# Batch 0's attention by head pairs: an order of work written out by hand in a fused attention and snake-MLP kernel

## The chip, the cores and the metric

The kernel runs on one core of a Trainium2 chip. Its time is the device time of one execution in microseconds (us); the median of four runs of the kernel before is 236.2 us, from 235.82 to 236.86. Lower is better.

## The reference

There are 4 batches, 8 heads, 768 tokens and 64 values per head. Each chunk of 32 queries attends to 8 memory slots, 16 keys to its left, its own 32 and 8 to its right. The 8 heads' outputs, side by side, are a 512-wide row per token, and a two-layer MLP with the activation h + sin(alpha h)^2 / alpha follows. All matrices come in float32; the result is 3072 x 512 float32.

```python
scores = scale * np.matmul(q_c, k_full.transpose(0, 1, 3, 2))
a = np.exp(scores - np.max(scores, axis=-1, keepdims=True))
a = a / (np.sum(a, axis=-1, keepdims=True) + 1e-09)
out[:, :, c_start:c_end] = np.matmul(a, v_full)
...
h = x @ w_in                       # 512 -> 2048
g = h + np.sin(alpha * h) ** 2 / (alpha + 1e-09)
return g @ w_out                   # 2048 -> 512
```

## The kernel before

Everything is in bf16 on the matmul side. The order on every engine is the order of the program text, since the schedule is manual.

A token block is 96 tokens (three chunks); a batch has NJ = 8 blocks. The 128 key rows of a block are the 112 keys around it with 8 memory rows between (partitions 64 to 71 of `vw`, columns 40 to 47 of each 104 in `kTi`). Heads go in 4 pairs, since two heads of 64 values fill 128 partitions.

Loading. All of q, k, v and the weights are loaded by DMAs issued on POOL, which convert to bf16 on the way. Batch 0's q and k come pair by pair (`load_qk_pair`, L100), v block by block with two DMAs each (`load_v`, L121), then the first-layer weights in five pieces, q and k of batch 1, the second-layer weights in two pieces, and v of batch 1 (`load_v_all`, L134). [...] an issue waits until the DMA eight places before it has landed. mem_k and alpha are loaded on SP's queue, mem_v on POOL's.

Transposes. `t_k` and `t_q` (L247, L260) turn a pair's k or q on the PE into a PSUM tile (`turn`, L236); DVE copies k into `kTi` (L249, L255), ACT copies q into `qT` (L262). `put_memk` and `put_memv` place the memory rows. For batch 0 the program (L418) does all four pairs, k and q in turn, with two filler matmuls (`spin`, L167: zeros times zeros, to keep the PE busy) after each.

Attention. `qk_exp(j)` (L266) scores one token block for all 8 heads, 8 matmuls into the two-bank tile `sc`, and takes exp on ACT in three parts of 32 queries (L279); the mask is the per-partition bias, which differs for the first and the last block. `pv` (L286) multiplies by v with a column of ones for the sums; DVE takes the reciprocal (L296) and multiplies (L297) into `x_blk`. `xt` (L304) transposes that block on the PE, and DVE or ACT copies it into `xT` (L313). `burst` (L316) runs the eight blocks one after the other, weighting two steps after scoring.

MLP. For each of 16 slices `ft` of 128 hidden values, `l1` (L339) makes 8 matmuls (L347), Sin on ACT (L359), a square on ACT, DVE or POOL by the letter in `sq` (L362, L368, L364), and a multiply-add on DVE into `gT` (L376). For ft 3, 7 and 11 of batch 0 the two halves go to single-bank tiles (`split`; L356, L372). DVE's part of slice ft is written after the matmuls of slice ft and ahead of those of ft + 1. `l2` (L382) is the second layer: 16 matmuls per 128 tokens (L404), a copy, a store. It is a generator, from which the next batch's attention and first layer take steps between their own (`stream.take`). In batch 0's first layer nothing of it runs yet. After that layer come batch 1's transposes (`pair_up`, L223, on POOL and DVE, then `t_k` and `t_q`).

PSUM has three two-bank buffers (`big`: scores, outputs, hidden tiles) and two one-bank buffers (`smp`: fillers, second-layer outputs, some transposes).

```python
for n in range(2 * HP):
    (t_k if n % 2 == 0 else t_q)(kq[n % 2], n // 2)
    spin(2)
...
sq = ("ADADADADPDPAADAA" if i == 0 else "ADAAPDADADAPADAD")[ft]
```

Of the kernel before, what the change touches and what calls it, by code (L numbers as in the profile page):

```python
# [9 lines left out]
P = 128  # L10
QW = 96
NEG = -30000.0
KW = 856
BF = mybir.dt.bfloat16
F32 = mybir.dt.float32
# [30 lines left out]
def kernel(  # L46
# [46 lines left out]
    memv_st = consts.tile([P, B, H, D], BF, name="memv_st")  # L93
    memk_f = gp.tile([32, H, D], F32, name="memk_f", tag="gT")
    w_in_sb = consts.tile([P, KT, d_ff], BF, name="w_in_sb")
    w_out_sb = consts.tile([P, FT, d_model], BF, name="w_out_sb")
# [23 lines left out]

    def load_v(b, j):  # L121
        vw = vws[b % 2]
        lo = QW * j - 16
        r0 = max(0, -lo)
        nc.gpsimd.dma_start(
            vw[r0:64, :, j, 0:D], v[b, :, lo + r0:lo + 64, :].rearrange("h p d -> p h d")
        )
        n = min(56, S - (QW * j + 48))
        nc.gpsimd.dma_start(
            vw[72:72 + n, :, j, 0:D],  # L130
            v[b, :, QW * j + 48:QW * j + 48 + n, :].rearrange("h p d -> p h d"),
        )

    def load_v_all(b):  # L134

        vw = vws[b % 2].rearrange("p h j c -> p (h j) c")
        vf = v[b].rearrange("h s d -> (h s) d")
        n = H * NJ
        nc.gpsimd.dma_start(
            vw[16:64, :, 0:D],  # L140
            vf.rearrange("(n p) d -> p n d", p=QW)[0:48])
        nc.gpsimd.dma_start(
            vw[72:120, :, 0:D],
            vf.rearrange("(n p) d -> p n d", p=QW)[48:96])
        nc.gpsimd.dma_start(
            vw[0:16, 1:n, 0:D],
            vf.rearrange("(n p) d -> p n d", p=QW)[80:96, 0:n - 1])
        nc.gpsimd.dma_start(
            vw[120:128, 0:n - 1, 0:D],
            vf.rearrange("(n p) d -> p n d", p=QW)[0:8, 1:n])  # L150

# [14 lines left out]

    def spin(n):  # L167

        z = smp.tile([P, 512], F32, name="z", tag="sm")
        for _ in range(n):  # L170
            nc.tensor.matmul(z[:], zeros[:, 0:P], zeros[:])  # L171
# [10 lines left out]
    masks.make_identity(nc, ident[:])  # L182
    for hp in range(1, HP):
        load_qk_pair(0, hp, *kq)
    for b in range(B):
        nc.sync.dma_start(memk_f[NM * b:NM * b + NM], mem_k[b].rearrange("h n d -> n h d"))
    nc.gpsimd.dma_start(memv_st[64:72].rearrange("n b h d -> n (b h) d"),
                        mem_v.rearrange("b h n d -> n (b h) d"))
    for c, (a, e) in enumerate(((0, 16), (16, 56), (64, 120), (120, P), (32, 96), (64, 72))):
# [7 lines left out]
    nc.scalar.copy(memk_bf[:], memk_f[:])  # L197
    for j in range(NJ):
        load_v(0, j)
    with nc.allow_non_contiguous_dma(reason="alpha transpose load"):  # L200
# [26 lines left out]

    state = {"n": 0, "t": 0, "pools": 3}

# [6 lines left out]
    def turn(src, hp):  # L236

        t = t_tile()
        for r in range(6):
            if src.shape[1] == 6:  # L240
                nc.tensor.transpose(t[:, r, :], src[:, r].rearrange("p e d -> p (e d)"), ident[:])  # L241
            else:
                for e in range(2):
                    nc.tensor.transpose(t[64 * e:64 * e + 64, r, :], src[:, 2 * hp + e, r, :], ident[:])
        return t
# [13 lines left out]

    def t_q(qb, hp):  # L260
        t = turn(qb, hp)
        nc.scalar.copy(  # L262
            qT[:, hp, :].rearrange("p (a r) -> p a r", r=6), t[:].rearrange("p r a -> p a r")
        )

    def qk_exp(j):  # L266
        sc = big.tile([P, 2, 512], F32, name="sc", tag="big")
        for hp in range(HP):
            for e in range(2):
                nc.tensor.matmul(  # L270
                    sc[:, e, QW * hp:QW * hp + QW],
                    kTi[64 * e:64 * e + 64, hp, 104 * j:104 * j + P],
                    qT[64 * e:64 * e + 64, hp, QW * j:QW * j + QW],
                )
        pt = pts[state["n"] % NPT]
        state["n"] += 1
        for m in range(3):
            col = ((1 if j == 0 else 0), 4, (2 if j == NJ - 1 else 3))[m]
            nc.scalar.activation(  # L279
                pt[:, 0:H * QW].rearrange("p (g e c) -> p e g c", g=4, e=2)[:, :, :, 32 * m:32 * m + 32],  # L280
                sc[:, :, 0:4 * QW].rearrange("p g (e c) -> p g e c", e=4)[:, :, :, 32 * m:32 * m + 32],
                ACTF.Exp, bias=biasm[:, col:col + 1], scale=0.125,
            )
        return pt

    def pv(b, j, pt):  # L286
        x_blk = blk.tile([QW, H, D], BF, name="x_blk")
        rinv = blk.tile([QW, H], F32, name="rinv")
        ot = big.tile([P, 2, 512], F32, name="ot", tag="big")
        otv = ot[:, :, 0:4 * (D + 1)].rearrange("p g (e c) -> p g e c", e=4)  # L290
        for h in range(H):
            nc.tensor.matmul(  # L292
                otv[:, h // 4, h % 4, :], pt[:, QW * h:QW * h + P], vws[b % 2][:, h, j, 0:D + 1]
            )
# [8 lines left out]

    def xt(xT, j, x_blk, ot):  # L304
        if ot is None:
            xtp = smp.tile([P, KT, QW], BF, name="xtp", tag="sm")[:]
        else:
            xtp = ot[:].bitcast(BF)[:, 0, 640:640 + KT * QW].rearrange("p (k c) -> p k c", k=KT)
        for kt in range(KT):
            nc.tensor.transpose(  # L310
                xtp[:, kt, :], x_blk[:, 2 * kt:2 * kt + 2, :].rearrange("p e d -> p (e d)"), ident[0:QW, 0:QW]
            )
        (nc.scalar.copy if ot is None and j in (4, 5, 6) else nc.vector.tensor_copy)(  # L313
            xT[:, :, QW * j:QW * j + QW], xtp)

    def burst(b, stream, shares, lag):  # L316

        xT = xp.tile([P, KT, S], BF, name="xT")
        ptl, xbl = {}, {}
        back = lag + (2 if b == 0 else 1)  # L320
        for s in range(NJ + back):
            n = shares[s] if s < len(shares) else 0
            if s < NJ:
                ptl[s] = qk_exp(s)
            if b == 0:
                spin(1 if 3 <= s < NJ else 2)
            stream.take(n // 3, True)
            if 0 <= s - lag < NJ:
                xbl[s - lag] = pv(b, s - lag, ptl.pop(s - lag))
                if b == 0:  # L330
                    xbl[s - lag] = (xbl[s - lag][0], None)
            stream.take((n + 1) // 3, True)
            if 0 <= s - back < NJ:
                xt(xT, s - back, *xbl.pop(s - back))
            stream.take((n + 2) // 3, True)
        return xT


    def l1(i, ft, xT, gT, sq, split=False):  # L339
        if split:  # L340
            hts = [smp.tile([P, 512], F32, name="hs", tag="sm") for _ in range(2)]
        else:
            hT = big.tile([P, 2, 512], F32, name="hT", tag="big")
            hts = [hT[:, 0], hT[:, 1]]
        for kt in range(KT):
            for hf in range(2):
                nc.tensor.matmul(  # L347
                    hts[hf][:, 0:HALF],
                    w_in_sb[:, kt, P * ft:P * ft + P],
                    xT[:, kt, HALF * hf:HALF * hf + HALF],  # L350
                    start=(kt == 0), stop=(kt == KT - 1),
                )
        u = mlp.tile([P, 2, HALF], F32, name="u")
# [63 lines left out]

    for n in range(2 * HP):  # L418
        (t_k if n % 2 == 0 else t_q)(kq[n % 2], n // 2)
        spin(2)  # L420
        if n == 1:
            mt = smp.tile([P, HP, 32], BF, name="mt", tag="sm")
            for hp in range(HP):
                nc.tensor.transpose(
                    mt[:, hp, :],
                    memk_bf[0:32, 2 * hp:2 * hp + 2, :].rearrange("p e d -> p (e d)"),
                    ident[0:32, 0:32])
            nc.vector.tensor_copy(memkT[:], mt[:])
            put_memk(0)
    put_memv(0)  # L430
    nc.vector.reciprocal(inv_alpha[:], alpha_sb[:])
    for c0, c1 in ((0, 256), (256, 512), (512, 1024), (1024, 1536), (1536, 2048)):
        load_w_in(c0, c1)
    kq_next = load_qk(1)
    for c in range(2):
        load_w_out(c)
    load_v_all(1)

    stream = Stream()
    xT = burst(0, stream, (), 2)  # L440
    put_memk(1)

    for i in range(B):
# [19 lines left out]
        for ft in range(FT):  # L463
            sq = ("ADADADADPDPAADAA" if i == 0 else "ADAAPDADADAPADAD")[ft]
            if 1 <= ft:
                stream.take(3 if last else 2)
            if 0 < i < B - 1 and ft in at_ft:
                piece(at_ft[ft])
            if i == 0 and ft == 13:
                pair_to(2)  # L470
            if finish is not None:
                finish()
            finish = l1(i, ft, xT, gT, sq, i == 0 and ft in (3, 7, 11))
        finish()
        stream.add(l2(i, gT, last))
        if not last:
# [16 lines left out]
            if i + 2 < B:  # L493
                load_v_all(i + 2)
                put_memv(i + 2)
# [31 lines left out]
```

## Time and profile before

| | us |
|---|---|
| Median of four runs | 236.2 |
| The profiled execution's own time | 236.38 |
| Its span in the trace | 234.5 |
| Batch 0: first scores on the PE (L270) | 15.24 |
| Batch 0: exps on ACT, first start to last end (L279) | 15.91 to 24.77 |
| Batch 0: first Sin of the first layer (L359) | 29.88 |
| Batch 0: last multiply-add of the first layer ends (L376) | 55.13 |
| Batch 1: first scores on the PE (L270) | 62.04 |

The profile is of one execution. A row of the timeline has the start, the length, the engine, the line, what is written and read, and in brackets the idle time before it with what ended that. In the chain of waits each row is a start, a length and a place, followed back from the last instruction to whatever released it. Granted clock of the PE is 1.0 throughout.

### The profile page before, as it was taken

The numbers are of one execution on the slowest core, as the hardware profiler recorded it, in microseconds if no ns is written. First come the engines' busy times: TensorE is split into PE (matmuls) and PEld (weight loads), VectorE is DVE, ScalarE is ACT, GpSimd is POOL, SyncE is SP. The second block draws the span as 40 slices with busy tenths as digits, with TensorE's granted clock in tenths as the row PEclk, the third lists the DMA queues.
The fourth block names the chain that finished last, engine by engine and source line by source line (L and its number), as shares of the span: only waits on it lengthen the run. The fifth ranks groups of instructions, "written<-read, shape, count | busy, mean of one in ns | idle before, by whom it ended". The sixth has DMA issues, their size and how long they took to land.

```text
span 234.5 us, 4580 instructions
## 1 busy us (share of the span) xinstructions
PE 221.4 (94%) x1841; PEld 122.5 (52%) x1841; DVE 160.4 (68%) x287; ACT 150.2 (64%) x235; POOL 74.0 (32%) x85
## 2 busy tenths in 40 slices
PE   7799999888999999999999999999999999899994
PEld 2345565445545565564455656564555555453453
DVE  5467659999847987988557698978566358775110
ACT  2359689774697297899664787779564676880110
POOL 8889951823942115139300115020000020110000
PEclk9999999999999999999999999999999999999999
DMA  6999999999999910019999101001111110101112
GB/s 69 176 123 88 156 200 203 207 207 128 141 224 194 122 45 0 3 46 139 186 144 107 45 0 48 0 8 39 45 48 45 48 46 0 45 0 48 65 69 89
DMA packets 52500, 21.07 MB, mean 90 GB/s; under 512 B 36480, under 2 KB 49536, under 8 KB 52480
## 3 DMA queue, kind: packets, MB, share of 16 engines
q0 software_dynamic: 46528, 14.43, 73.5%
q1 hardware_dynamic: 5952, 6.37, 8.7%
q8 instruction: 14, 0.23, 0.4%
q14 instruction: 6, 0.05, 0.1%
HBM read 28.91 MB, written 6.29 MB: 150 GB/s over the span
## 4 chain that ended last, share of the span: by engine, by line
PE 64%; DVE 16%; ACT 8%; issue 6%; DMA 2%; POOL 2%; POOLq 1%; DVEq 0%; ACTq 0%
PE o L404 30%; PE hT L347 18%; DVE gT L376 6%; DVE s L368 4%; ACT u L359 3%; PE sc L270 3%; PE ot L292 3%; DMA q_bf<-in_q_dram 2%; DVE x_blk L297 2%; ACT s L362 2%; PE z L171 2%; PE tt_a L241 2%; ACT pt L279 2%; POOL s L364 2%; PE ot L310 2%
## 5 line engine op out<-in xcount | busy, mean ns | idle before, releaser
L404 PE MATMUL o<-w_out_sb,gT 128*128 128x512 bf16 x368 | 98.5, 380 | 1.2 <-DMA w_out_sb<-in_moe_w_out_dram 0.7
L347 PE MATMUL hT<-xT,w_in_sb 128*128 128x384 bf16 x488 | 87.3, 326 | 4.2 <-DVE gT L376 3.8
L376 DVE SCALAR_TENSOR_TENSOR gT<-s,inv_alpha,hT 128x768 bf16<-128x768 f32 x61 | 60.9, 1012 | 23.1 <-ACT s L362 15.0
L359 ACT ACTIVATE u<-hT,alpha_sb 128x768 f32<-128x768 f32 x61 | 54.7, 897 | 25.4 <-PE hT L347 24.3
L347 PEld LDWEIGHTS <-w_in_sb 128*128 128x128 bf16 x512 | 49.3, 98 | 39.3 <-issue 4.9
L404 PEld LDWEIGHTS <-gT 128*128 128x128 bf16 x368 | 31.9, 97 | 27.1 <-DVE gT L376 1.2
L279 ACT ACTIVATE pt<-sc,biasm 128x256 bf16<-128x256 f32 x96 | 37.4, 488 | 12.8 <-PE sc L270 12.7
L364 POOL TENSOR_TENSOR s<-u 128x768 f32<-128x768 f32 x8 | 12.5, 1567 | 76.1 <-ACT u L359 65.8
L362 ACT ACTIVATE s<-u 128x768 f32<-128x768 f32 x32 | 27.0, 843 | 1.3 <-DVE gT L376 0.4
L368 DVE TENSOR_TENSOR s<-u 128x768 f32<-128x768 f32 x24 | 25.9, 1077 | 0.7 <-ACT u L359 0.5
L297 DVE TENSOR_TENSOR x_blk<-ot,rinv 96x512 bf16<-96x512 f32 x32 | 22.0, 687 | 1.1
L223 POOL COPY pr<-q_bf 128x768 bf16<-128x768 bf16 x12 | 10.2, 853 | 38.8 <-PE tt_a L241 25.3
L296 DVE RECIPROCAL rinv<-ot 96x8 f32<-96x8 f32 x32 | 6.4, 201 | 18.2 <-PE ot L292 18.0
L411 DVE COPY o_sb<-o 128x512 f32<-128x512 f32 x12 | 8.3, 688 | 15.5 <-PE o L404 15.4
L413 ACT COPY o_sb<-o 128x512 f32<-128x512 f32 x11 | 6.4, 583 | 17.9 <-PE o L404 17.9
L171 PE MATMUL z<-zeros 128*128 128x512 bf16 x45 | 15.4, 439 | 1.3 <-DVE zeros L165 1.2
L292 PEld LDWEIGHTS <-pt 128*128 128x128 bf16 x256 | 12.1, 97 | 7.5 <-issue 2.7
L292 PE MATMUL ot<-vw,pt 128*128 128x65 bf16 x256 | 13.0, 193 | 0.7 <-ACT pt L279 0.4
L270 PEld LDWEIGHTS <-kTi 64*128 64x128 bf16 x256 | 6.8, 94 | 12.4 <-issue 5.9
L241 PEld LDWEIGHTS <-pr 128*128 128x128 bf16 x144 | 10.1, 98 | 5.2
L270 PE MATMUL sc<-qT,kTi 64*128 64x96 bf16 x256 | 11.4, 205 | 0.8 <-DVE gT L376 0.6
L310 PEld LDWEIGHTS <-x_blk 96*128 96x128 bf16 x128 | 8.5, 97 | 6.0 <-issue 0.7
(70 smaller groups left out, 171.6 us busy)
## 6 DMA issues: line engine op xcount, KB each, us to landing
out_dram<-o_sb SPq DMA_DIRECT2D x23, 256.0 KB, 2.4
k_bf<-in_k_dram POOLq DMA_DIRECT2D x3, 768.0 KB, 9.3
q_bf<-in_q_dram POOLq DMA_DIRECT2D x3, 768.0 KB, 13.1
vw<-in_v_dram POOLq DMA_DIRECT2D x6, 384.0 KB, 17.4
w_out_sb<-in_moe_w_out_dram POOLq DMA_DIRECT2D x2, 1024.0 KB, 24.7
w_in_sb<-in_moe_w_in_dram POOLq DMA_DIRECT2D x3, 512.0 KB, 9.8
k_bf<-in_k_dram POOLq DMA_DIRECT2D x4, 192.0 KB, 5.8
q_bf<-in_q_dram POOLq DMA_DIRECT2D x4, 192.0 KB, 6.1
```

What stands on the lines that cost most here:

```text
L171: nc.tensor.matmul(z[:], zeros[:, 0:P], zeros[:])
L270: nc.tensor.matmul(sc[:, e, QW * hp:QW * hp + QW], kTi[64 * e:64 * e + 64, hp, 104 * j:104 * j + P], qT[64 * e:64 * e + 64, hp, QW * j:QW ...
L279: nc.scalar.activation(pt[:, 0:H * QW].rearrange("p (g e c) -> p e g c", g=4, e=2)[:, :, :, 32 * m:32 * m + 32], sc[:, :, 0:4 * QW].rearra ...
L292: nc.tensor.matmul(otv[:, h // 4, h % 4, :], pt[:, QW * h:QW * h + P], vws[b % 2][:, h, j, 0:D + 1])
L297: nc.vector.tensor_tensor(out=x_blk[:].rearrange("p (g e) d -> p g e d", g=2), in0=otv[0:QW, :, :, 0:D], in1=rv.unsqueeze(3).to_broadcast( ...
L347: nc.tensor.matmul(hts[hf][:, 0:HALF], w_in_sb[:, kt, P * ft:P * ft + P], xT[:, kt, HALF * hf:HALF * hf + HALF], start=(kt == 0), stop=(kt ...
L359: nc.scalar.activation(u[:], hT[:, :, 0:HALF], ACTF.Sin, scale=alpha_sb[:, ft:ft + 1])
L362: nc.scalar.activation(s2[:], u[:], ACTF.Square)
L364: nc.gpsimd.tensor_tensor(out=s2[:], in0=u[:], in1=u[:], op=ALU.mult)
L368: nc.vector.tensor_tensor(out=s2[:], in0=u[:], in1=u[:], op=ALU.mult)
L376: nc.vector.scalar_tensor_tensor(out=gv, in0=s2[:], scalar=inv_alpha[:, ft:ft + 1], in1=hT[:, :, 0:HALF], op0=ALU.mult, op1=ALU.add)
L404: nc.tensor.matmul(o[:], gT[:, ft, P * s:P * s + P], w_out_sb[:, ft, :], start=(ft == 0), stop=(ft == FT - 1),)
```

## The change

Batch 0 no longer runs block by block over all heads. Its 32 cells (4 pairs by 8 token blocks) are grouped into eight units: unit u holds pair u // 2 and token blocks 0 to 3 or 4 to 7. An order string names every step on the PE: `k`, `q` turn a pair, `s` scores and takes exp of a unit, `v` weights it, `x` transposes it, `z` is a number of fillers. The parts:

- v is loaded by pair, four DMAs per pair, with pair 0 ahead of q and k of pairs 2 and 3. The same function with all 64 rows serves the other batches. v of batch 1 is issued at ft 8 of batch 0's first layer instead of before it.
- mem_v is loaded as float32 on SP's queue and cast by ACT.
- q of pairs 1 and 3 is copied by DVE instead of ACT.
- Batch 0's turns stand in `smp` tiles, with the two fillers written into the same tile ahead of the transposes.
- Where the cells of a unit need different biases, an exp is issued in two parts.
- Batch 0's block transposes go into the free part of the unit's output tile; a unit's copy fills 384 tokens of one 128-row slice of `xT`. The last four copies are on ACT.
- The first layer's first slice takes its matmuls half by half (for batch 0 with the last slice of `xT` at the end).
- The squares of batch 0's first layer are placed anew; alpha's reciprocal comes after the attention.

```diff
+ORDER = (
+    "k 0,q 0,memk 0,k 1,s 0,q 1,s 1,memv 0,s 2,k 2,v 0,q 2,s 3,x 0,v 1,k 3,s 4,x 1,q 3,s 5,"
+    "z 1,v 2,s 6,x 2,z 1,v 3,s 7,x 3,z 2,v 4,z 2,v 5,x 4,z 1,v 6,x 5,z 1,v 7,x 6,z 1,x 7"
+)
...
+    def load_v(b, n0, n1):
         vw = vws[b % 2].rearrange("p h j c -> p (h j) c")
         vf = v[b].rearrange("h s d -> (h s) d")
+        vf = vf.rearrange("(n p) d -> p n d", p=QW)
+        for dst, src in (
+            (vw[16:64, n0:n1, 0:D], vf[0:48, n0:n1]),
+            (vw[72:120, n0:n1, 0:D], vf[48:96, n0:n1]),
+            (vw[0:16, n0 + 1:n1, 0:D], vf[80:96, n0:n1 - 1]),
+            (vw[120:128, n0:n1 - 1, 0:D], vf[0:8, n0 + 1:n1]),
+        ):
+            nc.gpsimd.dma_start(dst, src)
...
     load_qk_pair(0, 0, *kq)
     masks.make_identity(nc, ident[:])
-    for hp in range(1, HP):
+    load_qk_pair(0, 1, *kq)
+    load_v(0, 0, 16)
+    for hp in range(2, HP):
         load_qk_pair(0, hp, *kq)
...
-    nc.gpsimd.dma_start(memv_st[64:72].rearrange("n b h d -> n (b h) d"),
-                        mem_v.rearrange("b h n d -> n (b h) d"))
+    nc.sync.dma_start(memv_f[64:72].rearrange("n b h d -> n (b h) d"),
+                      mem_v.rearrange("b h n d -> n (b h) d"))
...
     nc.scalar.copy(memk_bf[:], memk_f[:])
-    for j in range(NJ):
-        load_v(0, j)
+    nc.scalar.copy(memv_st[64:72], memv_f[64:72])
+    for hp in range(1, HP):
+        load_v(0, 16 * hp, 16 * hp + 16)
...
     def turn(src, hp):
-        t = t_tile()
+        if src.shape[1] == 6:
+            t = t_tile()
+        else:
+            z = smp.tile([P, 512], F32, name="z", tag="sm")
+            spin(2, z)
+            t = z[:].bitcast(BF)[:, 0:6 * P].rearrange("p (r c) -> p r c", r=6)
...
-    def qk_exp(j):
+    def qk_exp(cells):
...
+            cols = [((1 if j == 0 else 0), 4, (2 if j == NJ - 1 else 3))[m] for _, j in cells]
+            c0 = 0
+            for c1 in range(1, 5):
+                if c1 < 4 and cols[c1] == cols[c0]:
+                    continue
+                nc.scalar.activation(
+                    pt[:, 0:H * QW].rearrange("p (g e c) -> p e g c", g=4, e=2)[:, :, c0:c1, 32 * m:32 * m + 32],
...
+                c0 = c1
...
+    def first_burst(kq):
+        xT = xp.tile([P, KT, S], BF, name="xT")
+        cells = [[(u // 2, 4 * (u % 2) + c) for c in range(4)] for u in range(8)]
+        ptl, xbl = {}, {}
+        for what, n in [t.split() for t in ORDER.split(",")]:
+            n = int(n)
+            if what == "k":
+                t_k(kq[0], n)
+            elif what == "q":
+                t_q(kq[1], n, nc.vector.tensor_copy if n in (1, 3) else nc.scalar.copy)
...
+            elif what == "s":
+                ptl[n] = qk_exp(cells[n])
+            elif what == "z":
+                spin(n)
+            elif what == "v":
+                xbl[n] = pv(0, cells[n], ptl.pop(n))
+            elif what == "x":
+                hf = n % 2
+                xt(xT[:, n // 2, HALF * hf:HALF * hf + HALF].rearrange("p (k c) -> p k c", k=KT),
+                   *xbl.pop(n), nc.vector.tensor_copy if n < 4 else nc.scalar.copy)
+        return xT
...
+        order = [(kt, hf) for kt in range(KT) for hf in range(2)]
+        if ft == 0 and i == 0:
+            order = [(kt, hf) for hf in range(2) for kt in range(KT - 1)] + [(KT - 1, 0), (KT - 1, 1)]
+        elif ft == 0:
+            order = [(kt, hf) for hf in range(2) for kt in range(KT)]
...
-    load_v_all(1)
...
-    xT = burst(0, stream, (), 2)
+    xT = first_burst(kq)
+    nc.vector.reciprocal(inv_alpha[:], alpha_sb[:])
...
-            sq = ("ADADADADPDPAADAA" if i == 0 else "ADAAPDADADAPADAD")[ft]
+            sq = ("ADAPADAPDADADAAA" if i == 0 else "ADAAPDADADAPADAD")[ft]
...
+            if i == 0 and ft == 8:
+                load_v(1, 0, H * NJ)
```

## The prediction

> **What bounds the kernel now.** I read the page's engine shares first, then the chain of waits over 0 to 70 us (the change touches only batch 0's front and first layer), then the timeline there, then the DMA issues.
>
> ```profile
> PE 221.4 (94%) x1841; PEld 122.5 (52%) x1841; DVE 160.4 (68%) x287; ACT 150.2 (64%) x235; POOL 74.0 (32%) x85
> ```
>
> The PE's 94% is an average. The chain, start and length in us, tells what rules the part concerned:
>
> ```profile
> 2.20 5.84 DMA q_bf<-in_q_dram
> ...
> 14.81 0.81 ACT qT L262
> ...
> 15.91 4.49 ACT pt L279 x12
> ...
> 24.43 0.69 DVE x_blk L297
> ...
> 28.53 1.33 PE hT L347 x7
> ...
> 44.73 1.95 DVE s L368
> ...
> 58.34 0.82 PE o L404 x3
> ```
>
> Five stages: transposes of all four head pairs until 14.8, eight exp blocks on ACT, a tail of weighting, transposing and copying until 28.5, the first layer (L1) that ends on DVE at 55.13, then batch 1's transposes, behind two kTi copies on DVE (57.29 to 58.29), until 58.34. After 62 us the chain is nearly all PE matmuls, so what reaches that point is kept. Timeline rows (start, length) of the ends of these stages:
>
> ```profile
> 15.91 8.86 ACT L279 ACTIVATE pt<-sc,biasm 128x256 bf16<-128x256 f32 x24 [0.31 <-PE sc L270]
> ...
> 29.88 0.90 ACT L359 ACTIVATE u<-hT,alpha_sb 128x768 f32<-128x768 f32 x1 [0.81 <-PE hT L347]
> ...
> 44.39 1.47 POOL L364 TENSOR_TENSOR s<-u 128x768 f32<-128x768 f32 x1 [0.71 <-ACT u L359]
> 44.65 2.02 DVE L368 TENSOR_TENSOR s<-u 128x768 f32<-128x768 f32 x1
> ...
> 54.12 1.01 DVE L376 SCALAR_TENSOR_TENSOR gT<-s,inv_alpha,hT 128x768 bf16<-128x768 f32 x1 [0.52 <-ACT s L362]
> ```
>
> Exp costs 0.369 each when packed (8.86/24); the last ends at 24.77, and 5.1 us pass until the first Sin, at 29.88: that tail is what can be shortened. The DVE square at 44.65 takes 2.02 where the group's median is 0.95: it started while POOL squared. The loads:
>
> ```profile
> k_bf<-in_k_dram POOLq DMA_DIRECT2D x4, 192.0 KB, 5.8
> vw<-in_v_dram POOLq DMA_DIRECT2D x7, 64.0 KB, 2.8
> vw<-in_v_dram POOLq DMA_DIRECT2D x7, 56.0 KB, 3.4
> ```
>
> By issue plus landing time, k and q land at 5.4, 8.0, 9.1, 10.1, 11.0, 12.0, 12.9, 14.0: 0.99 apart at the end. v's 16 DMAs go out at 8.6 to 21.9, about 0.7 of issue each, and land 2.7 later: POOL's issuing paces them, the engines don't. The first w_in lands at 26.6, the last w_out at 55.2, where PE waits 0.66 for it.
>
> [...] 2.02 against 0.95 above; three squares beside v issues (32.62, 106.69, 110.21) took 0.95. [...] The load here (27.79) is 1.28 and Sin waits for the PE, not for it; [...]
>
> **The change part by part.**
>
> *Loads.* v is now issued per head pair (4 DMAs), pair 0 ahead of k2, q2, k3, q3, and mem_v leaves POOL for SP. The queue never runs dry: each issue is 4 us ahead of its turn. The rate of v with a full queue I take from batch 1's v: 55.2 to 64.8, 9.6 us with a store among it, so 2.1 to 2.4 per pair; I take 2.3. From q1 at 10.1: v0 12.4, k2 13.4, q2 14.4, k3 15.4, q3 16.3, v1 18.6, v2 20.9, v3 23.2, w_in 24.5 (2.1 earlier), the last w_out about 53.2. POOL's waits for the DMA eight places back are met in time: v1's for v0 at 11 to 14.
>
> *mem_v's cast.* A copy of 8x2048 on ACT, ahead of q0's copy. [...] memk is cast by 6.4. The landing is not in the trace: mem_k's four DMAs on that queue have all landed by 4.46, alpha, issued at 2.20, takes 5.4 and lands at 7.6. I take 6, bounds 4.5 and 8.5. Then ACT is free at 8.3, before q0's copy at 8.6: nothing. On SP's queue alpha goes out 0.4 later, behind mem_v; it lands near 8 and is needed at 28.
>
> *Exps.* Blocks of one pair hold a first or last token block, so a bias differs and one exp of three is cut into 64 and 192 elements[...]. They start at 10.7 instead of 15.9 and I get the last at 22.9, so this is hidden.
>
> *The front.* I walk the written order with each engine in order: two fillers and a turn 0.43 + 0.46, scores 0.28, weighting 0.24, block transposes 0.17 on PE; on DVE k's copies 1.02, q's copy 0.87, mem_v 1.18, reciprocal and multiply 0.85, xT copy 0.27; q's copy 0.8 and xT's 0.48 on ACT (spacings in the timeline). DVE then ends k1 at 11.5, q1 12.5, mem_v 13.7; k2 (waits for its load) 15.0, block 0 15.9, block 1 17.4, k3 18.4, q3 19.6, block 2 20.5, block 3 22.3, then blocks 4 to 7 back to back from 23.4: 23.4 + 4 x 0.85 = 26.9. Block 7's transposes 27.1 to 27.4, its ACT copy until 27.9, table load 1.28: first Sin at 29.2, against 29.88: 0.7 gained. PE's ft 0 ends at 28.5, against 29.86; that 1.3 isn't all kept, because before, the load was hidden behind L1's first matmuls, and now it is last. If v takes 2.7 per pair, Sin is at 29.6; at 2.1, 29.1. DVE's waits in the walk are short but for one of 1.1 before block 4, so its 15 us of work after 9.8 is the limit, not the loads. Three edits cost nothing here: alpha's reciprocal (0.25) moves behind block 7, where DVE idles until 31; the fillers, fewer now, stand on PE where it waits anyway; ft 0's matmuls run half by half, six of them ahead of the last two blocks, and for later batches PE is busy throughout at that place (80.24).
>
> *L1 of batch 0.* The squares go from A8 D6 P2 to A9 D5 P2, with P at 3 and 7. From the first Sin (before 29.88), in us: multiply-add 3 ends at 7.8 before; now the POOL square starts at 5.3 + 0.1, takes 1.5, and DVE stands idle for it: 8.1. ft 7: 13.65 before; now 13.25. ft 9: 17.85 before, with the 2.02 square; now 16.15. ft 12: 20.8 before; now with D at 8, 10 and 12 21.1. ft 15's matmuls need ft 12's buffer: 21.1 + 1.35, then Sin, square, multiply-add: 25.4 against 25.25. So L1 gains 1.07 from the contention and gives it back: 0.15 lost. v of batch 1, issued at ft 8, costs POOL 4.3 us at about 41 to 46, after both its squares, and then it copies batch 1's k and q, needed only at 52; behind w_out in the queue anyway, it lands by 63 (needed at 67). The three DVE squares beside it cost nothing by the rows above, 1.07 if one starts inside a POOL copy.
>
> *Batch 1's transposes.* w_out's 0.66 wait goes, but the chain through 54 to 58.3 is DVE's: multiply-add, pr, kTi, pr, kTi. What is late next is that same DVE work. Of it, one pr copy took 0.98 (alone 0.45) as POOL's copy began 0.06 before it; with PE free to turn k1 right after the first pr, POOL is about 0.25 less in the way.
>
> Sum: -0.7 + 0.15 - 0.25 = -0.8. Against the profiled execution: 236.38 (span 234.5 and 1.9 around it) becomes 235.6; it lies 0.2 over the median of 236.2, so 235.4.
>
> **Rivals.** *Slower: mem_v's cast holds ACT.* q0's copy, then the scores, q1, every exp and DVE's whole walk stand behind it. From a landing of 6.8 on, each us costs one: at 8, the first Sin is at 30.4; at 8.5, 30.9, so 1.7 worse than forecast: 237.1. It decides from 7.6, where the 0.8 is gone. For it: alpha's 5.4 to land. Against it: mem_v has 256 pieces of 256 B, alpha 2048 of 4 B, and the last of mem_k's took under 2.7. *No change: L1 takes it back.* L1 is nearly DVE-bound; one more collision (1.07) or an idle wait for a POOL square that is 0.5 longer cancels the gain: 236.2. This is also the case that the pairs arrive early but DVE, not arrival, rules. *More.* If block 7's copy or the table load is less exposed (Sin at once after PE's 28.5) and ft 15 isn't held by its buffer, 0.5 + 0.6 more: 234.3.
>
> **How the numbers follow.** Forecast 0.47, slower 0.20, no change 0.20, more 0.13. A measurement of this kernel tells about 0.3%, 0.7 us, from no change. Of the forecast 0.30 is faster than that and 0.17 within; of no change 0.02, 0.13 and 0.05 slower. Faster 0.45, within 0.30, slower 0.25. Range 234.2 to 237.1: from the larger gain to the late cast.
>
> **What would show it.** Right: the first Sin near 29.2 directly behind a table load; mem_v's cast over by 8.5; DVE without gaps from 12 to 20 and 23 to 27; w_in landing near 24.5; no square near 2 us in L1; a DVE gap of about 1.2 before ft 3's multiply-add; no PE wait for w_out. Wrong: q0's copy waiting on ACT, k2 landing after 14, a Sin after 29.9, or a multiply-add of ft 15 ending more than 25.4 after the first Sin.

## The result, and the profile after

The kernel with the change is slower by half a per cent: 237.2 us as the median of 42 runs (236.03 to 238.77), against 235.97 for the kernel before in the same comparison; ratio 1.0048, interval 1.0036 to 1.006. The forecast was 235.4. (Below, as in the prediction, "block n" of the changed kernel is its unit n, and "q0" or "k1" is the q or k of a pair; times are in us.)

The runs of the kernel after fall into three groups by the granted clock of the PE, averaged over the execution:

| Mean granted clock, after | runs | median us |
|---|---|---|
| 0.997 to 1.0 | 19 | 236.47 |
| 0.991 to 0.993 | 14 | 237.47 |
| 0.984 to 0.985 | 9 | 238.38 |

Of the 103 runs of the kernel before that stand beside the experiments, 101 kept a mean clock of 0.997 or more; the medians of the three sets are 235.85 to 235.89. So there are two losses: about 0.5 at full clock, and 1.0 for each step of clock, which over half of the executions pay once or twice.

The profiled execution of after (236.24, span 234.4) is one at full clock. Its share of PE, and the chain of waits from 0 to 62 us:

```profile
PE 218.5 (93%) x1831; PEld 121.7 (52%) x1831; DVE 159.9 (68%) x287; ACT 153.3 (65%) x244; POOL 71.6 (31%) x84
```

```profile
2.19 5.41 DMA q_bf<-in_q_dram
...
10.91 0.60 PE z L160 x2
...
12.02 0.97 DVE qT L259
...
28.60 1.28 ACT L394
...
58.34 0.82 PE o L439 x3
```

PE has 2.9 us less to do: ten fillers are gone. Fillers (L160) lie on the chain, as they did before; the exps, 4.49 of the chain before, are off it, and the table load has come onto it. At 58.34 the second layer starts, the same figure as before. The timeline of the same places (start, length, and in brackets the idle time ahead and what ended it):

```profile
10.91 0.60 PE L160 MATMUL z<-zeros 128*128 128x512 bf16 x2 [0.91 <-DVE kTi L252]
```

```profile
28.60 1.28 ACT L394 ACT_TABLE_LOAD   x1
29.89 0.90 ACT L394 ACTIVATE u<-hT,alpha_sb 128x768 f32<-128x768 f32 x1
...
36.65 1.14 DVE L407 SCALAR_TENSOR_TENSOR gT<-s,inv_alpha,hs 128x384 bf16<-128x384 f32 x2 [1.02 <-POOL s L399]
...
54.34 1.01 DVE L411 SCALAR_TENSOR_TENSOR gT<-s,inv_alpha,hT 128x768 bf16<-128x768 f32 x1 [1.51 <-ACT s L397]
```

The first Sin is at 29.89 (29.88 before), directly behind the table load, and the last multiply-add of L1 ends at 55.35 (55.13). That looks like no change at all, but the two executions did not start alike: in the profiles here the first loads land up to 0.9 apart. Batch 0's first transpose of q, which waits for its data, starts at 8.09 in the profile before and at 7.65 after. From there the lengths can be compared:

| us | q0 to first Sin | first Sin to end of L1 | end of L1 to batch 1's scores | sum |
|---|---|---|---|---|
| before | 21.79 | 25.25 | 6.91 | 53.95 |
| after | 22.24 | 25.46 | 6.70 | 54.40 |

After minus before is 0.45, and the medians at full clock differ by 0.5 to 0.6: the sums speak for the medians, where the two spans did not. The first length scatters by about 0.3: the front of before, unchanged in two experiments below, took 21.79, 21.79 and 22.09 in three profiles. Behind batch 1's first scores (62.04 and 62.05) the two traces run alike.

The loads did what they were meant to. The issues of 0 to 30 us, with each one's KB and the median from issue to landing:

```profile
k_bf<-in_k_dram POOLq DMA_DIRECT2D x4, 192.0 KB, 5.2
q_bf<-in_q_dram POOLq DMA_DIRECT2D x4, 192.0 KB, 5.4
vw<-in_v_dram POOLq DMA_DIRECT2D x8, 96.0 KB, 4.9
```

No turn of k or q waits for its DMA after q0's, and PE's wait for w_out at 55 is gone.

### The profile page after: what moved, and what is told of

Read it like the earlier page. It is cut to its first block, busy times and chain, and to the rows that moved or that the text cites. A ratio compares the mean times of both kernels' runs of the same rounds, so it can differ in the third digit from the quotient of the medians.

```text
span 234.4 us, 4575 instructions
## 1 busy us (share of the span) xinstructions
PE 218.5 (93%) x1831; PEld 121.7 (52%) x1831; DVE 159.9 (68%) x287; ACT 153.3 (65%) x244; POOL 71.6 (31%) x84
## 4 chain that ended last, share of the span: by engine, by line
PE 65%; DVE 17%; ACT 6%; issue 6%; DMA 2%; POOL 1%; POOLq 1%; DVEq 0%; ACTq 0%
PE o L439 30%; PE hT L382 20%; DVE gT L411 6%; PE sc L266 3%; DVE s L403 3%; ACT u L394 3%; DVE x_blk L299 3%; PE ot L294 3%; PE ot L309 2%; DMA q_bf<-in_q_dram 2%; PE tt_a L238 2%; ACT s L397 2%; PE o L428 1%; PE z L160 1%; DVE kTi L246 1%
## 5 line engine op out<-in xcount | busy, mean ns | idle before, releaser
L279 ACT ACTIVATE pt<-sc,biasm 128x256 bf16<-128x256 f32 (+2 forms) x104 | 39.2, 463 | 14.5 <-PE sc L266 14.3
L399 POOL TENSOR_TENSOR s<-u 128x768 f32<-128x768 f32 x8 | 11.7, 1464 | 83.1 <-ACT u L394 61.3
L397 ACT ACTIVATE s<-u 128x768 f32<-128x768 f32 x33 | 27.8, 843 | 1.0
L138 POOL DMA_DIRECT2D vw<-in_v_dram x28 | 24.6, 888 | 0.1
L403 DVE TENSOR_TENSOR s<-u 128x768 f32<-128x768 f32 x23 | 23.8, 1037 | 0.7 <-ACT u L394 0.5
L160 PE MATMUL z<-zeros 128*128 128x512 bf16 x35 | 12.3, 458 | 2.4 <-DVE zeros L153 1.2
L309 PE MATMUL ot<-ident,x_blk 96*128 96x96 bf16 x128 | 10.8, 206 | 2.6 <-DVE x_blk L299 2.5
```

The costliest lines, as they stand in the source:

```text
L138: nc.gpsimd.dma_start(dst, src)
L279: nc.scalar.activation(pt[:, 0:H * QW].rearrange("p (g e c) -> p e g c", g=4, e=2)[:, :, c0:c1, 32 * m:32 * m + 32], sc[:, :, 0:4 * QW].re ...
L309: nc.tensor.transpose(xtp[:, kt, :], x_blk[:, 2 * kt:2 * kt + 2, :].rearrange("p e d -> p (e d)"), ident[0:QW, 0:QW])
L397: nc.scalar.activation(s2[:], u[:], ACTF.Square)
L403: nc.vector.tensor_tensor(out=s2[:], in0=u[:], in1=u[:], op=ALU.mult)
```

## The experiments

The same lengths for all of them in us, from one profile each, with the time's median (4 to 22 runs) and its ratio to the runs of before that stand beside it. The profiled executions of e1, e3, e4 and e8 lost clock. e9 to e12 ran on another chip, with their own runs of before.

| | q0 to Sin | L1 | to scores | sum | us | ratio (interval) |
|---|---|---|---|---|---|---|
| e1_after_again | 23.16 | 25.48 | 6.69 | 55.33 | 237.32 | 1.007 (1.0053 to 1.0086) |
| e2_gap_fill | 22.30 | 25.46 | 6.69 | 54.45 | 236.36 | 1.0023 (1.0014 to 1.0032) |
| e3_no_fill | 23.85 | 26.23 | 6.70 | 56.78 | 238.34 | 1.0108 (1.0092 to 1.0124) |
| e4_before_no_fill | 23.27 | 25.25 | 6.69 | 55.21 | 237.55 | 1.0049 (1.0018 to 1.008) |
| e5_mt_big | 22.54 | 25.45 | 6.70 | 54.69 | 236.57 | 1.003 (1.0019 to 1.0041) |
| e6_x7_dve | 21.81 | 25.90 | 6.69 | 54.40 | 236.52 | 1.0014 (1.0004 to 1.0025) |
| e7_mt_x7 | 22.12 | 25.88 | 6.70 | 54.70 | 236.65 | 1.004 (1.0026 to 1.0054) |
| e8_before_sq | 22.09 | 28.20 | 6.69 | 56.98 | 238.82 | 1.0142 (1.0112 to 1.0171) |
| e9_old_squares | 22.41 | 24.44 | 6.70 | 53.55 | 235.54 | 0.9982 (0.9971 to 0.9993) |
| e10_x7_squares | 21.95 | 23.56 | 6.69 | 52.20 | 234.11 | 0.9913 (0.9889 to 0.9938) |
| e11_before_squares | 21.79 | 23.56 | 8.41 | 53.76 | 235.95 | 1.0011 (0.9984 to 1.0039) |
| e12_early_k2 | 21.45 | 23.56 | 7.20 | 52.21 | 234.56 | 0.9952 (0.9924 to 0.998) |

### The clock: e1 to e4

The first theory: the clock is what the change costs, since its front leaves PE idle. The rival: the path itself is longer.

**e1_after_again** is the kernel after, unchanged, to catch an execution that loses the clock.

> The changed kernel once more, for the clock of each execution. Theory C (clock): the granted PE clock is lost in steps, because the front leaves the PE idle more often; the executions fall into groups at mean clock 1.00, 0.992 and 0.985 with 236.3, 237.3 and 238.4 us. Rival P (path): the front or the first layer is longer by itself; then executions at clock 1.00 are also about 1 us slower than the kernel before (237.2 against 236.0).

All four runs lost clock (0.992, 0.985, 0.992, 0.992). The profile shows where, first the page's rows of 40 slices of the span (tenths of busy time of the PE, then of its granted clock; 9 is 90% or more), then stretches of 1.5 us (start and end, length, busy time of PE, weight loads, DVE, ACT, POOL, each with a number of instructions; then the granted clock, the DMA share and GB/s):

```profile
PE   7788799979999999998999999998999999899994
PEclk9979999999999999999999999999999999999999
```

```profile
9.00:10.50 1.50, 1.25 (x22) 0.58 (x21) 0.62 (x2) 0.47 (x2) 0.73 (x2) 1.00 2.25 151
10.50:12.00 1.50, 0.84 (x14) 0.42 (x14) 0.60 (x3) 1.15 (x4) 0.93 (x2) 1.00 1.53 189
12.00:13.50 1.50, 0.72 (x24) 0.52 (x18) 1.21 (x2) 0.96 (x3) 1.50 (x3) 0.94 1.31 200
13.50:15.00 1.50, 1.50 (x17) 0.52 (x14) 0.97 (x1) 1.50 (x6) 1.50 (x2) 0.50 1.57 187
...
16.50:18.00 1.50, 1.50 (x34) 1.01 (x34) 1.00 (x5) 0.61 (x1) 1.50 (x4) 0.92 1.65 102
```

The kernel before, in the first three of these stretches:

```profile
9.00:10.50 1.50, 1.50 (x27) 0.87 (x28) 1.08 (x3) 0.45 (x1) 1.19 (x3) 1.00 1.27 185
10.50:12.00 1.50, 1.50 (x28) 0.72 (x22) 0.60 (x4) 0.80 (x1) 1.22 (x2) 1.00 1.30 197
12.00:13.50 1.50, 1.50 (x26) 0.73 (x25) 0.92 (x3) 0.68 (x1) 0.95 (x3) 1.00 1.76 165
```

From 9 to 13.5 PE is busy 2.8 of 4.5 us, in before all of it; then the clock is half for about 3.4 us (0.18 + 3.0 + 0.24), in which PE is "busy" throughout because the matmuls take longer: 17 of them fill 13.5 to 15, 24 in after's profile, and eight scores at half clock take 0.50 (e3, at 9.58) against 0.34 (after, at 9.66). Half clock for 3.4 of 235 us is the step of 0.007 in the mean, and the front is 0.9 longer than in the full-clock profile of the same kernel (23.16 against 22.24).

That profile has the same 2.8 of 4.5 and kept its clock, so the busy share alone does not decide. By the same stretches of 1.5 us, the half clock lasts 3.42 in e1 (13.32 to 16.74), and in the two kernels with fewer fillers below 10.23 (e4, 21.33 to 31.56) and 23.88 (e3, 8.58 to 32.46): about one, three and seven times the same length. What starts it is not shown, and it is no plain threshold of the busy share: in e4 PE is busy 1.24 of 3.0 from 16.5 to 19.5, and the clock stays full until 21.33.

**e2_gap_fill** adds 18 fillers where PE stood idle (`f n` in the order puts n of them into the tile of the next scores), and puts block 1's scores ahead of q1's turn; nothing else. The diff shows a part of the order.

```diff
-    def qk_exp(cells):
+    def qk_exp(cells, fill=0):
         sc = big.tile([P, 2, 512], F32, name="sc", tag="big")
+        spin(fill, sc[:, 0])
...
-    "k 1,s 0,q 1,s 1,memv 0,s 2,k 2,v 0,q 2,s 3,x 0,v 1,..."
+    "k 1,s 0,f 3,s 1,q 1,memv 0,f 3,s 2,k 2,v 0,q 2,s 3,z 2,x 0,v 1,..."
```

> The changed kernel with filler matmuls put where the PE waits anyway (scores of unit 1 ahead of q1). Theory C: every execution at clock 0.999 to 1.00, median 236.2, within 0.3 of it, and the first Sin within 0.3 of 29.9. Rival P: clock plays no part, median stays at 237.2 or grows by what the fillers delay.

All 11 runs keep 0.998 to 1.0, at 236.36, which is after's full-clock group (236.47). The stretches of its profile, 9 to 13.5 us:

```profile
9.00:10.50 1.50, 1.50 (x25) 0.77 (x23) 0.71 (x2) 1.01 (x3) 0.74 (x2) 1.00 2.23 154
10.50:12.00 1.50, 1.50 (x24) 0.68 (x22) 0.45 (x3) 1.50 (x5) 1.45 (x2) 1.00 1.54 191
12.00:13.50 1.50, 1.20 (x18) 0.55 (x13) 1.31 (x2) 0.74 (x3) 1.35 (x4) 1.00 1.30 198
```

So work that computes nothing is worth 0.8 in the median here, and costs the path nothing that shows: q0 to Sin is 22.30 against 22.24. That it is the fillers and not the exchanged scores is shown by e5 below, which has the fillers with q1's turn back in its place: all 12 runs keep 0.998 or more.

**e3_no_fill** takes all fillers out of after's attention, the `z` of its order too (the ten at the start stay); **e4_before_no_fill** does so in the kernel before.

```diff
# e3
-            spin(2, z)
# e4
-            if b == 0:
-                spin(1 if 3 <= s < NJ else 2)
```

> The changed kernel without fillers in batch 0's attention (the ten at the start stay). Theory C: mean clock 0.985 or below in nearly all executions, median 238 or more. Rival P, with fillers on the path: the chain of waits has 3.5 us of fillers in the front, so the first Sin comes 1 to 2 us earlier and the median is 236 or less.

> The kernel before, without the fillers in its eight blocks (those between the transposes stay). Theory C: it loses the clock as the changed kernel does, mean 0.985 to 0.992, 237 to 238.4, so the cause is idle PE time and not the order by pairs. Rival P: ACT sets the pace of the blocks, the fillers are free, 235.9 to 236.2.

The clock rows, of e3 and of e4:

```profile
PEclk9755579999999999999999999999999999999999
```

```profile
PEclk9998589999999999999999999999999999999999
```

Without fillers the change's front runs at half clock from about 8.6 to 32.5 us (mean 0.95) and takes 238.34. In before the fillers of the block loop matter too: half clock from 21.3 to 31.6, 237.55. (e4 keeps the fillers between the transposes, so the two don't compare one to one.) Front and clock hang together in both kernels; as they are written, the front by pairs is the more exposed one, with 23 of 42 runs below 0.997 against 2 of 103. The theory of the clock stands for 0.7 of the 1.2 in the median. It does not explain why nothing was gained at full clock.

### The front at full clock: e5 to e7

All that follow, but for those made from before, start from e2_gap_fill, so that the clock is nearly out of the question (two of e7's 17 runs lose a step).

**e5_mt_big**: memk's transposes go to the large pool, and q1's turn is back ahead of block 1's scores.

```diff
-                mt = smp.tile([P, HP, 32], BF, name="mt", tag="sm")
+                mt = big.tile([P, HP, 32], BF, name="mt", tag="big")
...
-    "k 0,q 0,memk 0,k 1,s 0,f 3,s 1,q 1,memv 0,f 3,s 2,k 2,..."
+    "k 0,q 0,memk 0,k 1,s 0,q 1,f 3,s 1,memv 0,f 3,s 2,k 2,..."
```

> The kernel of e2_gap_fill, but memk's transposes use a tile of the large PSUM pool, so that the turns of pairs 0 and 1 alternate between the two small tiles and q1's turn need not wait until k1 has been copied out; q1's turn is back ahead of block 1's scores. Theory W (the front's forecast gain was eaten by q1's turn, which waited 0.91 for k1's tile, and by DVE's walk behind it): k1's fillers no longer wait for memkT, q1's copy on DVE starts near 11.1 instead of 12.16, and everything behind it on DVE moves up by 0.6 to 1.0; first Sin at 29.1 to 29.5 against 30.04, time 235.5 to 235.9 against 236.36. Rival L (the loads rule: k2 lands just before it is used): PE waits for k2's DMA at about 13.5, DVE stands idle there, Sin stays at 29.9 to 30.1, time 236.3.

A miss: the first Sin is at 30.16. Counted from q0, q1's copy on DVE came 0.41 earlier (4.01 against 4.42), as the theory has it, but k2's copy came 0.25 later (7.06 against 6.81). The rival is out as well: PE did not wait for k2's data. The rows of PE and DVE:

```profile
13.58 0.60 PE L160 MATMUL z<-zeros 128*128 128x512 bf16 x2
14.11 0.53 PE L241 MATMUL z<-ident,k_bf 128*64 128x128 bf16 x12
```

```profile
12.62 1.22 DVE L141 COPY vw<-memv_st 8x4096 bf16<-8x4096 bf16 x1
14.68 0.86 DVE L246 COPY kTi<-z 128x672 bf16<-128x672 bf16 x1 [0.85 <-PE z L241]
```

DVE is ready at 13.84 and idles 0.85 for k2's transposes, which stand on PE behind six fillers that I had left ahead of two blocks' scores. This is the other half of the fillers' lesson: put in a real gap they are free, put ahead of the next turn they are the path.

**e6_x7_dve**: block 7's copy on DVE, so that the table load does not wait for it.

```diff
-                   *xbl.pop(n), nc.vector.tensor_copy if n < 4 else nc.scalar.copy)
+                   *xbl.pop(n), nc.vector.tensor_copy if n < 4 or n == 7 else nc.scalar.copy)
```

> The kernel of e2_gap_fill with one edit: block 7's last copy runs on DVE instead of ACT, so that ACT's last copy is block 6's (ends at 27.9) and the table load can run beside block 7's transposes and copy. Theory T (block 7's copy and the table load stand in series at the end of the front and cost their full 0.48 + 1.28): the load runs from 27.9 to 29.2, the first Sin starts at 29.2 instead of 30.04, and as L1 keeps its length, the time falls by 0.8 to 235.5. Rival (something else is due at the same time: PE's first layer or DVE's copy): Sin at 29.7 or later, time 236.1 or more.

The front did gain (21.81 against 22.30), but L1 took 0.44 back, and the time is the rival's, within 0.2 of e2's. ACT's rows:

```profile
27.80 1.28 ACT L398 ACT_TABLE_LOAD   x1
29.44 0.90 ACT L398 ACTIVATE u<-hT,alpha_sb 128x768 f32<-128x768 f32 x1 [0.36 <-PE hT L386]
```

Sin now waits for PE, whose first matmul of L1 starts 20.31 after q0 in both kernels. Counted from q0, the multiply-add of ft 0 is still 0.49 earlier than in e2, that of ft 3 0.35 and that of ft 7 0.05. All of the loss shows in DVE's waits for the two POOL squares: 1.17 instead of 1.02 at ft 3, and 0.58 instead of 0.28 at ft 7. What holds back the Sins ahead of ft 7's square I did not settle.

**e7_mt_x7** has both edits.

> Both edits of e5_mt_big and e6_x7_dve in one kernel. If they are two separate pieces of one path, the gains add: first Sin at 28.4 to 28.7, time 234.7 to 235.1, faster than before (236.0). If the front is held by something that neither touches (loads, ACT's exps), the sum is that of the larger one: Sin at 29.2, time 235.5.

The gains do not add, and none shows in the time: front 22.12, L1 25.88, 236.65. With the front better and L1 no shorter, L1 was the next thing to try.

### The first layer's squares: e8 to e11

**e8_before_sq**: the kernel before with the change's order of squares.

```diff
-            sq = ("ADADADADPDPAADAA" if i == 0 else "ADAAPDADADAPADAD")[ft]
+            sq = ("ADAPADAPDADADAAA" if i == 0 else "ADAAPDADADAPADAD")[ft]
```

> The kernel before with nothing but the new order of squares in batch 0's first layer (A9 D5 P2 instead of A8 D6 P2). By the prediction the 2.02 square goes (1.07 less), but ft 3's multiply-add waits for an early POOL square and ft 12's comes later: the last multiply-add ends 25.4 after the first Sin (25.25 before), time within 0.3 of before. Rival (the new order is worth the collision alone): 24.2 to 24.6 after the first Sin, time 0.6 to 1.0 below before. Other rival: it is worse without v's late issue, over 25.8 and 0.5 above.

The second rival, and far beyond its bound: L1 takes 28.20, the time 238.82. Three of the six runs lose a step of clock, the profiled one inside L1 (21 matmuls from 41.52 take 4.64 there, where 24 from 33.32 take 4.06); the three at full clock take 238.65 to 238.77, so the clock is not the cause. POOL's rows, then DVE's:

```profile
36.21 0.84 POOL L148 DMA_DIRECT2D vw<-in_v_dram  x1 [1.83 <-DMA w_in_sb<-in_moe_w_in_dram]
37.07 1.48 POOL L364 TENSOR_TENSOR s<-u 128x768 f32<-128x768 f32 x1
```

```profile
38.58 1.14 DVE L372 SCALAR_TENSOR_TENSOR gT<-s,inv_alpha,hs 128x384 bf16<-128x384 f32 x2 [3.23 <-POOL s L364]
```

An early POOL square stands in POOL's queue behind batch 1's v, whose issues wait for earlier DMAs to land: 0.78, 1.20 and 1.83 for pieces of w_in. (In before too: from 10.31 to 14.27 five issues of v wait 0.25 to 0.30 each, for the q or k issued eight places before.) That is what moving v to ft 8 buys the change: it makes the early squares possible.

**e9_old_squares**: e2 with before's order of squares, and v of batch 1 at ft 11, behind them.

```diff
-            sq = ("ADAPADAPDADADAAA" if i == 0 else ...)[ft]
+            sq = ("ADADADADPDPAADAA" if i == 0 else ...)[ft]
-            if i == 0 and ft == 8:
+            if i == 0 and ft == 11:
                 load_v(1, 0, H * NJ)
```

> The kernel of e2_gap_fill with the squares' order of before (A8 D6 P2, POOL at ft 8 and 10), and batch 1's v issued at ft 11, behind both POOL squares, instead of at ft 8. Theory S (the new order of squares costs L1 about 0.5 against its start on PE: 27.45 from ft 0's first matmul to the last multiply-add after the change, 26.93 before): the last multiply-add ends at 55.0 to 55.2 instead of 55.50, time 0.3 to 0.5 less than e2's 236.36. Rival (L1 hangs on the first Sin, and the order of squares is neutral, as the prediction has it): 55.3 to 55.5, time within 0.15 of e2's.

L1 is 24.44, 1.02 shorter than with the change's order, and the time is 235.54, just under before. (Its loads came 0.3 late, so its absolute ends are later than expected; the lengths are not touched by that.) No DVE square took 2.02 here. POOL's squares did stretch, from 1.47 to 2.30 and 2.23; in each case a DVE square began within 0.05 of them:

```profile
41.97 2.30 POOL L403 TENSOR_TENSOR s<-u 128x768 f32<-128x768 f32 x1 [14.51 <-ACT u L398]
45.28 2.23 POOL L403 TENSOR_TENSOR s<-u 128x768 f32<-128x768 f32 x1 [1.01 <-ACT u L398]
...
41.99 0.95 DVE L407 TENSOR_TENSOR s<-u 128x768 f32<-128x768 f32 x1
45.23 0.95 DVE L407 TENSOR_TENSOR s<-u 128x768 f32<-128x768 f32 x1
```

DVE waited 0.18 and 0.24 for them, against 1.02 and 0.28 with the squares at ft 3 and 7. The order and v's place were changed together; no run separates them.

**e10_x7_squares** is e6 (and so has e2's fillers) with a third order and v at ft 11; **e11_before_squares** is before with that order and nothing else.

```diff
-            sq = ("ADAPADAPDADADAAA" if i == 0 else ...)[ft]
+            sq = ("DADADAADADPAADAA" if i == 0 else ...)[ft]
```

> The kernel of e6_x7_dve (first Sin at 29.44) with another order of squares, DADADAADADPAADAA: one POOL square, late, with no DVE square beside it, D at ft 0 and two pairs of A; batch 1's v at ft 11. Theory S2 (in L1 the sharing of squares decides, DVE's waits for POOL and their collisions first of all): from a walk with the trace's durations the last multiply-add ends at 53.1 to 53.6 instead of 55.34, and the time falls by 1.7 to 2.2 to 234.3 to 234.8. Rival (L1 is bound by DVE's sum of work or by PE, whoever squares): 54.8 or later, time 235.9 or more.

> The kernel before with nothing but the order of squares of e10_x7_squares. Its one POOL square is late (ft 10), after POOL has issued batch 1's v at 37.6, so that the wait of e8_before_sq can't come back. Theory S2: last multiply-add at 53.4 to 53.9 instead of 55.13, time 1.2 to 1.7 below before: 234.3 to 234.8. So the better order would be worth as much without the change. Rival: w_out or batch 1's loads are due then (w_out's second half lands at 55.2 in before): PE waits for it up to 55.2, and only 0 to 0.5 is kept.

L1 is 23.56 in both, 1.7 less than before and 1.9 less than after. As e11 has no other edit, the order alone does it. In e10 it is all kept: 234.11, ratio 0.9913, faster than both kernels. In e11 it is not: 235.95. PE's waits from 27 to 70 us of e11 (us in total, times, longest):

```profile
PE o L404 <- DMA w_out_sb<-in_moe_w_out_dram: 2.5, 1, 2.5
```

The second half of w_out lands at 55.4 there (55.2 before), and 4 of its 14 runs lose a step of clock besides. Here the change's load order pays: w_out lands at 52.7 in e10, soon enough that PE doesn't wait for it.

**e12_early_k2** is e10 with memk's tile as in e5, and two fillers ahead of k2's turn where e5 has six.

```diff
-    "k 0,q 0,memk 0,k 1,s 0,f 3,s 1,q 1,memv 0,f 3,s 2,k 2,..."
+    "k 0,q 0,memk 0,k 1,s 0,q 1,s 1,memv 0,f 2,s 2,k 2,..."
```

> The kernel of e10_x7_squares with memk's transposes in the large PSUM pool as in e5_mt_big, but with two fillers instead of six ahead of k2's turn. Theory F (in e5_mt_big q1's copy came 0.53 earlier on DVE and the gain was lost because six fillers stood on PE ahead of k2's turn): k2's copy on DVE starts at 13.7 to 14.0 (14.68 in e5), the whole walk behind it moves up by 0.7, ft 0 starts on PE at 27.3 instead of 27.94, time 0.5 to 0.7 below e10's. Rival (k2 lands at about 14): PE waits for k2's DMA, no gain. Risk: with fewer fillers some executions lose the clock, 0.8 per step.

The theory of the front holds: k2's copy starts at 14.03, q0 to Sin is 21.45, 0.50 less than e10 and 0.34 less than before, the only front here that is below all three profiles of before's. The time did not follow: PE waits 1.2 for w_out, which lands at 53.3, and the sum is e10's (52.21 and 52.20). And the risk came true: 4 of 13 runs are at 0.993, with 236.42 to 237.43; the other nine are at 233.63 to 235.18, with a median of 234.11. Those with a step took about 2.3 longer, where 0.8 was expected.

## Why the prediction was wrong

Forecast: 0.7 gained in the front, 0.15 lost in L1, 0.25 gained at batch 1. Measured: 0.45 lost, 0.21 lost, 0.21 gained, and then the clock, 0.7 in the median. So two steps failed: the walk of the front, by 1.15, and the price of the fillers, by 0.7.

**The fillers, 0.** The step is this: "the fillers, fewer now, stand on PE where it waits anyway", costed at nothing. As PE time that was right; e2 shows that 18 more cost nothing either. Wrong was to ask only what the fillers cost and not what they are for. The granted clock was in the page of the kernel before, as a row of nines, and the prediction gave it no place. What they are for shows in the runs: without them all four of e3 lost clock (0.949 to 0.950), with 18 more all eleven of e2 kept it (0.998 to 1.0). No single long idle stands ahead of it: in e1, from 9 to 13.5, where before's PE was busy throughout, no wait is longer than 0.9, but together they leave PE busy 2.8 of 4.5 us, and half clock follows at 13.32. Why after's own profile, with the same 2.8 of 4.5, kept its clock, no run shows.

**The front, -0.7.** This is the larger error. The walk of engines said that DVE ends k1's copies 3.4 and q1's copy 4.4 behind the start of q0's transposes (11.5 and 12.5); they ended 3.2 and 5.3 behind it (12.98 for q1's). So most of the error arises at that one place, and all of it stays: the walk let q1's turn run while k1 was copied, but PE's fillers of q1 waited 0.91 for k1's copies to end. (Those of k1 waited 0.31 for memkT, without making k1 late against the walk.) At the end of block 7 the lag is 1.2, and the first Sin is 1.1 later than forecast. e12 shows that a front by pairs can be shorter: with those waits cut and k2's turn early, and with e6's edit, it is 0.34 shorter than before's. Waits of 0.60 and 0.73 for k1's copies remain in e5 and e12, with memk's tile out of the way, so that tile wasn't the only cause; what else ties q1's turn to k1's copies I did not settle (in after, the turns of q2 and q3 don't wait for k2's and k3's copies). I can't say either how much of the remaining 0.4 they hold.

**Table load at the end of the front.** The walk had it exposed behind block 7's ACT copy, and it is (1.28 at 28.60, Sin at 29.89). e6 shows that, with this order of squares, taking block 7's copy off ACT brings the first Sin 0.49 forward and the end of L1 not at all; what it is worth with e10's order no run shows.

**L1, +0.15.** Measured from Sin, 25.46 against a forecast of 25.4: right, and right on the way (ft 12's multiply-add ends at 21.1, as forecast). DVE's gap ahead of ft 3 (1.02) and no square of 2 us were also as forecast. But the sum hid a bad trade: in this kernel before's own order of squares, with v at ft 11, gives 24.44 (e9), 1.0 less. The prediction took the 2.02 of before as bound to that order. It hung on a few tenths: before's second POOL square began 0.26 ahead of a DVE square, in e9 it began 0.05 behind it.

**Batch 1, -0.25.** Right in size, 0.21: the second pair copy took 0.76 instead of 0.98. e4 and e8, made from before, end L1 later, so that PE doesn't wait for w_out, and have the same 0.76 and 6.69: it was w_out's wait that made the 0.98, as the prediction had it. "What is late next is that same DVE work" held, until L1 got 1.7 shorter: in e11 and e12 w_out took its place.

**The rival that was to be slower, mem_v's cast.** Its data landed near 6.8, the cast took 1.89 (the prediction's 8.3 leaves it 1.9 behind memk's 6.4), ended at 8.73 and held q0's copy for 0.55, which the prediction had named as a sign of being wrong. But it cost nothing there: block 0's scores started at 9.66, right behind k1's transposes. So the time came out on that rival's side, for another reason.

## What to carry to other kernels

Before filler work is thinned out, or work is rearranged so that PE waits in short pieces, look at PE's busy share per few us and at the granted clock of many runs, not of the one that was profiled; a profile at full clock can hide a loss that most executions pay (23 of after's 42). Fillers belong into gaps that exist, never ahead of the next real turn (six there kept DVE idle for 0.85 in e5). When two profiles are compared to tenths, count from an event that marks the first data, and ask of any stage that gets shorter what is due at its end: here the same 1.7 in L1 were worth nothing in one kernel and all in the other, by when w_out landed.

## What the runs showed of the hardware

In five pairs of overlapping squares on DVE and POOL, one of the two took longer. In before DVE's took 2.02 instead of 0.95 when POOL's had begun 0.26 ahead of it; POOL's took 1.88 instead of 1.47 when DVE's had begun 0.39 ahead (e10), and 2.23 when it had begun 0.05 ahead (e9), while DVE's stayed at 0.95. In these three it was the one that began later. In the other two, whose starts are closer, it was not: at 41.40 in before and at 41.97 in e9 the POOL square stands 0.01 and 0.02 ahead of the DVE square, and it was POOL's that took 2.29 and 2.30. Beside issues of v no DVE square took longer (0.95 at 32.62, 106.69 and 110.21 in before). For one that starts inside a POOL copy the prediction had 1.07 more; a case of it in e8 took less: the DVE square at 45.13, inside POOL's copy from 44.76 to 45.58, took 1.25, 0.30 more than 0.95.

The clock was at half for 3.42 us in e1, 10.23 in e4 and 23.88 in e3, and after's times cluster by their mean clock (medians of 236.47, 237.47 and 238.38, 1.0 and 0.9 apart). The price of a step isn't fixed: it was 1.0 in after, the runs of e12 with one step took about 2.3 longer than those without, and two runs of e4 with two steps (mean clock 0.985) took 235.62 and 236.30, about as long as before. A spread of that form is a sign to look at the clock rather than at noise.
